# Linear attention with a gated feed-forward, one core: nine tokens per partition, no remainder tiles, 64x64 key-value products, and a new order of all engines

## The chip, the core and the metric

The kernel runs on one core of a Trainium2 chip. The metric is the time of one execution in microseconds of device time. Three timed runs of the kernel before gave 260.96, 260.99 and 261.04 us, median 260.99.

A core has five engines with a queue each: TensorE (PE, matrix products; the loading of its weights is listed apart as PEld), VectorE (DVE), ScalarE (ACT), GpSimd (POOL) and SyncE (SP). A queue runs its instructions in order; an instruction waits at its head until what it needs is there. Transfers are issued from SP, ACT or POOL, and all run on the same 16 DMA engines. Matrix products go to PSUM, which only PE, DVE and ACT reach; everything else lies in SBUF, 128 partitions wide.

## The reference, cut to what matters

```python
# q, k, v: (8 batches, 8 heads, 576 tokens, 64), f32
def phi(x):
    return np.where(x > 0, x, np.exp(x) - 1.0) + 1.0
q_p, k_p = phi(q), phi(k)
kv = np.einsum('bhsd,bhse->bhde', k_p, v)
z = np.sum(k_p, axis=2)
num = np.einsum('bhsd,bhde->bhse', q_p, kv)
den = np.einsum('bhsd,bhd->bhs', q_p, z)[..., None] + 1e-06
x = (num / den).transpose(0, 2, 1, 3).reshape(4608, 512)
a = x @ w1            # (512, 1024)
b = x @ w2            # (512, 1024)
h = a * b @ w3        # (1024, 1024)
out = h @ w_out       # (1024, 512)
```

Both kernels compute phi(x) as max(x + 1, min(exp(x), 1)) or, what is the same, min(exp(x), max(x, 0) + 1). Both multiply w3 and w_out first, into one 1024x512 matrix, so that each token takes three products instead of four: a, b and (a*b) @ (w3 @ w_out). All products are taken in bf16 with f32 sums.

## The kernel before, in words

**Tiles.** The 576 tokens of a batch are cut into 512, four to a partition (`NJ = 4`, tiles "J" of 128 tokens), and a remainder of 64 (`R`, tiles "R"; two batches share one). So q, k and v of a batch come as one load of 1 MB each and, for the remainder, two small loads of 64 KB each (`load_qkv`, L105; L111 is the small ones, L120 the large). The 4608 tokens make 36 tiles of 128; four tiles, whatever batch they are from, are a chunk of 512 tokens, and nine chunks go through the feed-forward.

**Attention, per batch.** `phi_exp` (ACT, L137), `phi_min` and `phi_max` (DVE, L141 and L162) make phi of q and k in bf16, in pieces of 1024 and 256 elements and, for the remainder, pieces of its own. `v_unit` (L171, L176) casts v into a tile with a column of ones beside each head, so that one product gives kv and z. `kv_half` (L181) multiplies for a pair of heads the two halves of the partitions separately (64 rows by 128 columns of the array, 130 columns moving), and DVE adds the two halves (L204). `kv_full` (L208) does the same at full height, for batch 0. `q_tr` (L302) transposes q on PE for batches 0 to 3, `qt_load` (L232) by a transposing transfer on SP for the others, and for the remainders. `nat_units` (L244) multiplies each transposed q tile with kv, head by head at half height (64 rows), takes the reciprocal of the denominators and scales (L271, L273, L275). The result is brought into the layout that the feed-forward needs, features on partitions, by `xt_tr` on PE (batches 1 and 3) or `xt_load` on SP. Batch 0 goes another way: `first_kvz` spreads kv and z into two block matrices, `first_nd` multiplies them with transposed q, 512 tokens at once, so that the result needs no transposing, and the reciprocal is taken on ACT as exp(-ln(x)).

**Feed-forward, per chunk.** `f_unit` (L379): for each of eight blocks of 128 features, four products into a_ps and four into b_ps (L371); ACT copies a_ps (L376), DVE multiplies with b_ps into ab (L377). `o_unit` (L386): eight products per tile of 128 tokens (L390), a copy on ACT or DVE (L393), and `o_store` on SP. `o_last` does the last tile in two halves (L417 to L420).

**Weights.** `load_w3`, `load_wo` and `load_w12` are issued from POOL and change f32 to bf16 on the way. `w3_tr` transposes w3 on PE (L454, copy L455), `wf_mm` multiplies with w_out (L464, copy L467).

**Order.** Nothing is scheduled by a program: `ORDER` (L470) is a list of steps, and each step appends its instructions to its engines' queues. `GATES` names six loads that wait for another one to be issued first. Letters: L, M, N load k, q, v; x, X exp; y, Y min; z, Z max; v cast; K kv; T, D transposing transfers; a, b transposes of q; A `nat_units`; P `xt_tr`; c to g, h, i, r the way of batch 0; E, C, B load w3, w_out, w1 and w2; w transposes w3; U, W multiply it with w_out; F, O, S, Q the feed-forward and its stores; a "+" moves a copy from ACT to DVE, or a load from SP to POOL. PSUM has eight banks: four for the feed-forward (tag "mm"), two tiles of two banks for attention ("at").

Of the kernel before, what the change touches and what calls it, by code (L numbers as in the profile page):

```python
# [13 lines left out]
P = 128  # L14
NCH = 512


@with_exitstack
def kernel(
# [10 lines left out]
):  # L30
    nc = tc.nc
    B, H, S, D = q.shape
    DM = H * D
    NTOK = B * S
# [3 lines left out]
    NJ = 4  # L38
    R = S - NJ * P
    JW = H * NJ * D  # L40
    RW = (H // 2) * D
    n_chunks = NTOK // NCH

    tile_of, order = {}, []
    for b in range(0, B, 2):
        for key in [("J", b, j) for j in range(NJ)] + [("J", b + 1, j) for j in range(NJ)] + [("R", b, 0)]:
            tile_of[key] = len(order)
            order.append(key)  # L50
        tile_of["R", b + 1, 0] = tile_of["R", b, 0]
# [5 lines left out]
    ldr = ctx.enter_context(tc.tile_pool(name="ldr", bufs=8))  # L57
    setup = ctx.enter_context(tc.tile_pool(name="setup", bufs=2))
    phi_p = ctx.enter_context(tc.tile_pool(name="phi", bufs=1))
    e_p = ctx.enter_context(tc.tile_pool(name="e", bufs=2))  # L60
    att = ctx.enter_context(tc.tile_pool(name="att", bufs=2))
    lr = ctx.enter_context(tc.tile_pool(name="lr", bufs=2))
# [5 lines left out]

    ident = consts.tile([P, P], BF16)
    mask = consts.tile([P, 2, 2, D], BF16)  # L70
# [5 lines left out]
    wo_sb = wpool.tile([P, FC, DM], BF16)  # L76
    wf_sb = wpool.tile([P, FC, DM], BF16)
    xt = wpool.tile([P, NT, KC, P], BF16)
    vt = wpool.tile([P, NJ, H, D + 1], BF16)
    vr = wpool.tile([P, H // 2, D + 1], BF16)  # L80

    def constants(part):
        if part == 0:
            make_identity(nc, ident)
        elif part == 1:

            nc.gpsimd.memset(mask, 0.0)
            nc.gpsimd.memset(mask[0:D, :, 0, :], 1.0)
            nc.gpsimd.memset(mask[D:P, :, 1, :], 1.0)
            nc.gpsimd.memset(eps, 1e-6)  # L90
            nc.gpsimd.memset(vt[:, :, :, D:D + 1], 1.0)
            nc.gpsimd.memset(vr[:, :, D:D + 1], 1.0)
        else:
            nc.vector.memset(zero, 0.0)

    def warm_up(n):

        ps = mm_ps.tile([P, NCH], F32, tag="mm", name="warm")
        for _ in range(n):
            nc.tensor.matmul(ps, zero[:, 0:P], zero, start=True, stop=True)  # L100


    raw = {}

    def load_qkv(name, src, b, part, alt=False):  # L105


        if part == 3:
            t = raw[name + "r", b] = ldr.tile([P, RW], F32, tag="ldr", name=f"{name}32r")
            for hh in range(2):  # L110
                (nc.gpsimd if alt else nc.sync).dma_start(  # L111
                    out=t[hh * R:(hh + 1) * R].rearrange("p (h d) -> p h d", d=D),
                    in_=src[b, hh * 4:(hh + 1) * 4, NJ * P:S, :].rearrange("h p d -> p h d"))
            return None
        if (name, b) not in raw:
            raw[name, b] = ld.tile([P, JW], F32, tag="ld", name=f"{name}32")
        t = raw[name, b]
        h0, h1 = ((0, 4), (4, 8), (0, 8))[part]
        W = NJ * D
        return nc.sync.dma_start(  # L120
            out=t[:, h0 * W:h1 * W].rearrange("p (h x) -> p h x", x=W),
            in_=src[b, h0:h1, 0:NJ * P, :].rearrange("h (p j) d -> p h (j d)", j=NJ))


    ph = {}

    es = {}

    def phi_exp(name, b, g):

        if g == 2:
            x, e = raw[name + "r", b], e_p.tile([P, RW], BF16, tag="er", name="er")
        else:
            x = raw[name, b][:, g * (JW // 2):(g + 1) * (JW // 2)]
            e = e_p.tile([P, JW // 2], BF16, tag="e", name="e", bufs=4)
        es[name, b, g] = x, e
        nc.scalar.activation(out=e, in_=x, func=AF.Exp)  # L137

    def phi_min(name, b, g):
        e = es[name, b, g][1]  # L140
        nc.vector.tensor_scalar_min(out=e, in0=e, scalar1=1.0)  # L141

    def phi_max(name, b, hp):

        if (name, b) not in ph:
            ph[name, b] = [None, None]
        if hp == KC:
            dr = ph[name, b][1] = phi_p.tile([P, RW], BF16, tag=name + "r", name=name + "r", bufs=3)
            todo = [(dr, *es[name, b, 2])]
        else:  # L150
            if hp == 0:
                ph[name, b][0] = phi_p.tile([P, KC, NJ, 2, D], BF16, tag=name + "j", name=name + "j")
            dj = ph[name, b][0]
            x, e = es[name, b, hp // 2]
            W = NJ * D
            todo = []
            for u in range(2):
                h = 2 * (hp % 2) + u
                todo.append((dj[:, hp, :, u, :], *(t[:, h * W:(h + 1) * W].rearrange(
                    "p (j d) -> p j d", d=D) for t in (x, e))))  # L160
        for out, x, e in todo:
            nc.vector.scalar_tensor_tensor(  # L162
                out=out, in0=x, scalar=1.0, in1=e, op0=ALU.add, op1=ALU.max)

    def copy_of(alt):
        return nc.vector.tensor_copy if alt else nc.scalar.copy

    def v_unit(b, i, alt=False):

        if i < 2:  # L170
            copy_of(alt)(  # L171
                out=vt[:, :, 4 * i:4 * i + 4, 0:D],
                in_=raw["v", b].rearrange("p (h j d) -> p j h d", h=H, j=NJ)[
                    :, :, 4 * i:4 * i + 4])
        else:
            copy_of(alt)(out=vr[:, :, 0:D], in_=raw["vr", b].rearrange("p (h d) -> p h d", d=D))  # L176


    kvs, qts, xns = {}, {}, {}

    def kv_half(b, g):  # L181


        kj, kr = ph["k", b]
        if g == 0:
            kvs[b] = att.tile([P, KC, 2, D + 1], BF16, tag="kv", name="kv")
        kvp = at_ps.tile([P, 2, 512], F32, tag="at", name="kvp")
        W = 2 * (D + 1)
        for i in range(2):
            hp = 2 * g + i  # L190
            steps = [(kj[:, hp, j].rearrange("p u d -> p (u d)"),
                      vt[:, j, 2 * hp:2 * hp + 2, :].rearrange("p h e -> p (h e)"), (0, 1))
                     for j in range(NJ)]
            steps.append((kr[:, i * P:(i + 1) * P],
                          vr[:, 2 * i:2 * i + 2, :].rearrange("p h e -> p (h e)"), (g,)))
            for n, (kk, vv, halves) in enumerate(steps):
                for r in halves:
                    rows = slice(r * R, (r + 1) * R)
                    nc.tensor.matmul(  # L199
                        kvp[:, r, i * W:(i + 1) * W], kk[rows], vv[rows],  # L200
                        start=(n == 0), stop=(n == (NJ if r == g else NJ - 1)))
        kvf = lr.tile([P, 2 * W], F32, tag="kvf", name="kvf")
        nc.scalar.copy(out=kvf, in_=kvp[:, 0, 0:2 * W])  # L203
# [4 lines left out]
    def kv_full(b, g):  # L208

        kj, kr = ph["k", b]  # L210
        if g == 0:
            kvs[b] = att.tile([P, KC, 2, D + 1], BF16, tag="kv", name="kv")
# [418 lines left out]
```

## Time and profile before

| | us |
|---|---|
| median of three runs | 260.99 |
| span of the profiled execution, first to last instruction | 258.1 |
| PE busy | 237.4 (92%) |
| DVE busy | 167.9 (65%) |
| ACT busy | 129.0 (50%) |
| POOL busy | 21.1 (8%) |
| 576 products of a and b | 150.0 |
| 266 recorded products of o | 63.2 |
| w3 @ w_out, 61 recorded products | 16.7 |
| HBM read, written | 38.80 MB, 9.44 MB |

The profiled execution's own time is told only by its span; the median of the runs lies 2.9 us above it. Busy time is the time in which at least one instruction of the group was running: products overlap in the pipeline, so a product of 512 columns is listed at 380 ns and costs 216 ns in a group. The granted clock was 0.999 over the span. The forty slices of section 2 of the page are 6.45 us each. In the table of stretches a row is: stretch, its length, then for each engine busy time and, in brackets, instructions, in the order PE, PEld, DVE, ACT, POOL (or the one engine asked for), then the granted clock, the DMA share and GB/s written.

### The profile page before, as it was taken

The page shows a single profiled execution, that of the slowest core. Times are in us where ns is not written, and L with a number is a line of the kernel's source. Part 1 is how long each engine was busy: PE and PEld are TensorE (multiplying, and loading weights), DVE is VectorE, ACT ScalarE, POOL GpSimd, SP SyncE. Part 2 cuts the span into 40 slices and gives each one's busy share as a digit, 9 for nine tenths or more (in the row PEclk, how much of TensorE's full clock was granted, in tenths as well). Part 3 has the DMA queues.
Part 4 walks back from the last instruction along what each step waited for, and adds up shares of the span by engine and source line. Part 5 has one row for each costly group of instructions (what it writes and reads, how often), then busy time and mean ns, then how long its engine had stood idle before and what let it go on. Part 6 is the DMA issues. An engine that isn't in the chain of part 4 may idle for free.

```text
span 258.1 us, 4507 instructions
## 1 busy us (share of the span) xinstructions
PE 237.4 (92%) x1656; PEld 116.2 (45%) x1673; DVE 167.9 (65%) x426; ACT 129.0 (50%) x205; POOL 21.1 (8%) x42
## 2 busy tenths in 40 slices
PE   1138999999999999999999999999999999999994
PEld 1124554545454454455444444444444444444442
DVE  0025787969978979997968589468866543423320
ACT  2048587858478664677353645726533203331421
POOL 8000765000101000000000000000000000000000
PEclk9999999999999999999999999999999999999999
DMA  6999999999898599939988975934980124003024
GB/s 100 200 257 378 316 229 245 208 334 307 302 291 250 87 340 215 307 104 253 211 193 245 369 160 123 248 99 131 218 220 26 34 57 124 0 37 125 3 82 163
DMA packets 70085, 48.98 MB, mean 190 GB/s; under 512 B 34416, under 2 KB 64368, under 8 KB 70064
## 3 DMA queue, kind: packets, MB, share of 16 engines
q1 hardware_dynamic: 63104, 42.54, 61.4%
q0 software_dynamic: 6816, 6.03, 14.1%
q8 instruction: 13, 0.21, 0.3%
q10 hardware_dynamic: 144, 0.13, 0.1%
q14 instruction: 8, 0.07, 0.1%
HBM read 38.80 MB, written 9.44 MB: 187 GB/s over the span
## 4 chain that ended last, share of the span: by engine, by line
PE 84%; DMA 8%; ACT 2%; SPq 1%; issue 1%; DVE 1%; DVEq 0%; POOLq 0%
PE a_ps L371 25%; PE b_ps L371 24%; PE o_ps L390 23%; DMA k<-in_k_dram 4%; DMA w3b<-in_moe_w_dram 4%; PE kvp L199 3%; PE wf_ps L464 3%; PE nd L265 3%; SPq L111 1%; PE tp L309 1%; PE w3p L454 1%; PE xtp L285 1%; PE o_ps L417 1%; DVE qj L162 1%; ACT e L137 0%
## 5 line engine op out<-in xcount | busy, mean ns | idle before, releaser
L371 PEld LDWEIGHTS <-w_sb 128*128 128x128 bf16 x576 | 54.2, 98 | 63.4 <-issue 0.5
L377 DVE TENSOR_TENSOR ab<-a_sb,b_ps 128x512 bf16<-128x512 f32 x72 | 49.0, 684 | 46.6 <-PE b_ps L371 35.4
L371 PE MATMUL a_ps<-xt,w_sb 128*128 128x512 bf16 x288 | 75.1, 380 | 0.1
L371 PE MATMUL b_ps<-xt,w_sb 128*128 128x512 bf16 x288 | 74.9, 379 | 0.0
L376 ACT COPY a_sb<-a_ps 128x512 f32<-128x512 f32 x72 | 41.9, 586 | 56.8 <-PE a_ps L371 55.6
L390 PE MATMUL o_ps<-wf_sb,ab 128*128 128x512 bf16 x266 | 63.2, 379 | 0.7
L390 PEld LDWEIGHTS <-ab 128*128 128x128 bf16 x280 | 26.7, 98 | 30.8
L393 ACT COPY o_sb<-o_ps 128x512 f32<-128x512 f32 x24 | 14.0, 583 | 30.7 <-PE o_ps L390 30.7
L162 DVE SCALAR_TENSOR_TENSOR kj<-k,e 128x256 bf16<-128x256 f32 x64 | 23.6, 417 | 0.1
L162 DVE SCALAR_TENSOR_TENSOR qj<-q,e 128x256 bf16<-128x256 f32 x64 | 23.4, 417 | 0.1
L141 DVE TENSOR_SCALAR e<-e 128x1024 bf16<-128x1024 bf16 x32 | 13.4, 420 | 14.2 <-ACT e L137 14.2
L137 ACT ACTIVATE e<-q 128x1024 bf16<-128x1024 f32 x16 | 16.7, 1058 | 9.3 <-DMA q<-in_q_dram 9.1
L454 PE MATMUL w3p<-ident,w3b 128*128 128x128 bf16 x64 | 6.1, 253 | 15.0 <-ACT w3t L455 8.0
L137 ACT ACTIVATE e<-k 128x1024 bf16<-128x1024 f32 x16 | 16.9, 1056 | 4.1 <-DMA k<-in_k_dram 2.7
L275 DVE TENSOR_TENSOR xn<-nd,r 128x512 bf16<-128x512 f32 x28 | 18.0, 686 | 0.0
L464 PE MATMUL wf_ps<-wo_sb,w3t 128*128 128x512 bf16 x61 | 16.7, 412 | 1.0 <-ACT w3t L455 0.8
L454 PEld LDWEIGHTS <-w3b 128*128 128x128 bf16 x64 | 4.9, 113 | 16.6 <-DMA w3b<-in_moe_w_dram 8.2
L393 DVE COPY o_sb<-o_ps 128x512 f32<-128x512 f32 x11 | 7.6, 688 | 6.4 <-PE o_ps L390 6.4
L171 ACT CAST vt<-v 128x1024 bf16<-128x1024 f32 x9 | 9.3, 1046 | 2.0 <-DMA v<-in_v_dram 2.0
L203 ACT COPY kvf<-kvp 128x260 f32<-128x260 f32 x14 | 5.3, 375 | 8.9 <-PE kvp L199 8.7
L464 PEld LDWEIGHTS <-w3t 128*128 128x128 bf16 x64 | 6.2, 104 | 7.8 <-issue 1.7
L199 PE MATMUL kvp<-vt,kj 64*128 64x130 bf16 x224 | 9.2, 217 | 0.0
(81 smaller groups left out, 163.5 us busy)
## 6 DMA issues: line engine op xcount, KB each, us to landing
out_dram<-o_sb SPq DMA_DIRECT2D x31, 256.0 KB, 3.2
k<-in_k_dram SPq DMA_DIRECT2D x7, 1024.0 KB, 8.6
q<-in_q_dram SPq DMA_DIRECT2D x7, 1024.0 KB, 8.2
v<-in_v_dram SPq DMA_DIRECT2D x6, 1024.0 KB, 7.4
w3b<-in_moe_w_dram POOLq DMA_DIRECT2D x8, 256.0 KB, 7.1
v<-in_v_dram SPq DMA_DIRECT2D x4, 512.0 KB, 8.5
w_sb<-in_moe_w_dram POOLq DMA_DIRECT2D x8, 256.0 KB, 11.3
out_dram<-o_sb SPq DMA_DIRECT2D x9, 128.0 KB, 2.4
```

The costliest lines, as they stand in the source:

```text
L137: nc.scalar.activation(out=e, in_=x, func=AF.Exp)
L141: nc.vector.tensor_scalar_min(out=e, in0=e, scalar1=1.0)
L162: nc.vector.scalar_tensor_tensor(out=out, in0=x, scalar=1.0, in1=e, op0=ALU.add, op1=ALU.max)
L199: nc.tensor.matmul(kvp[:, r, i * W:(i + 1) * W], kk[rows], vv[rows], start=(n == 0), stop=(n == (NJ if r == g else NJ - 1)))
L275: nc.vector.tensor_tensor(out=dst.rearrange("p (c u) e -> p u c e", u=2), in0=v4[:, :, :, 0:D], in1=r[0:n].unsqueeze(3).to_broadcast([n, 2 ...
L371: nc.tensor.matmul(ps, w[:, kc, f * P:(f + 1) * P], xt[:, 4 * c:4 * c + 4, kc, :], start=(kc == 0), stop=(kc == KC - 1))
L376: nc.scalar.copy(out=a_sb, in_=a_ps)
L377: nc.vector.tensor_mul(out=abs_[c][:, f, :], in0=a_sb, in1=b_ps)
L390: nc.tensor.matmul(o_ps, ab[:, f, m * P:(m + 1) * P], wf_sb[:, f, :], start=(f == 0), stop=(f == FC - 1))
L393: copy_of(alt)(out=o_sb, in_=o_ps)
L454: nc.tensor.transpose(tp[:, kc, :], raw["w3", i][:, kc * P:(kc + 1) * P], ident)
L464: nc.tensor.matmul(wfs[i], w3ts[i][:, kc, :], wo_sb[:, kc, :], start=(kc == 0), stop=(kc == FC - 1))
```

## The change

- **Nine tokens per partition.** 576 = 64 x 9: a batch's tokens lie on 64 partitions, nine in each, and the two heads of a pair on the two halves. There are no remainder loads; a partition's run is 2304 bytes. phi works on 1152 elements at a time: `phi_exp` on ACT, `phi_lin` (max(x, 0) + 1) and `phi_min` on DVE.
- **64x64 kv.** `kv_mm` gives each head and half its own quarter of the array; no halves are added afterwards. `kv_copy` puts kv on the diagonal of a block matrix whose rest is zero.
- **Full-height products.** `nat_mm` multiplies 128 rows with the block matrix, two heads at once.
- **One load queue.** All q, k and v loads are issued from POOL, in line with the weights; SP has only the transposing transfers and the stores. There are no gates.
- **Batches 0 and 1** take the direct way (`q_tr`, `kvz_copy`, `first_mm`, `first_recip`, `first_mult`), now in quarters of the array; the others get q transposed on SP, by halves (`q_load`), and x too (`x_load`); `xt_tr` is gone.
- A tile of 128 tokens now has two tokens of each of 64 partitions, so `f_mul` writes ab with the two interleaved, and a tile is stored by two transfers of 64 rows.
- **New order**, in finer steps: products, copies and the multiplication of the feed-forward are steps of their own, and 45 warm-up products (H) instead of 9 stand in it.

```diff
-    NJ = 4
-    R = S - NJ * P
+    NJ = 9
+    R = S // NJ
+    HW = NJ * D
+    NG = 4
...
-        return nc.sync.dma_start(
-            out=t[:, h0 * W:h1 * W].rearrange("p (h x) -> p h x", x=W),
-            in_=src[b, h0:h1, 0:NJ * P, :].rearrange("h (p j) d -> p h (j d)", j=NJ))
+        (nc.gpsimd if pool else nc.sync).dma_start(
+            out=raw[name, b][:, hs, :],
+            in_=src[b].rearrange("(hp u) (p j) d -> (u p) hp (j d)", u=2, j=NJ)[:, hs, :])
...
+    def phi_lin(name, b, c):
+        rs[name, b, c] = e_p.tile([P, 2, HW], BF16, tag="r", name="r", bufs=2)
+        nc.vector.tensor_scalar(
+            out=rs[name, b, c], in0=raw[name, b][:, 2 * c:2 * c + 2, :],
+            scalar1=0.0, scalar2=1.0, op0=ALU.max, op1=ALU.add)
+
+    def phi_min(name, b, c):
...
+        nc.vector.tensor_tensor(
+            out=ph[name, b][:, c].rearrange("p j a d -> p a j d"),
+            in0=es[name, b, c].rearrange("p a (j d) -> p a j d", j=NJ),
+            in1=rs[name, b, c].rearrange("p a (j d) -> p a j d", j=NJ), op=ALU.min)
...
+    def kv_mm(b, cs):
...
+        for c in cs:
+            for j in range(NJ):
+                for u in range(2):
+                    rows = slice(u * R, (u + 1) * R)
+                    for a in range(2):
+                        nc.tensor.matmul(
+                            kvps[b][a * D:(a + 1) * D, u, c * (D + 1):(c + 1) * (D + 1)],
+                            kk[rows, c, j, a, :], vt[rows, c, j, a, :],
+                            start=(j == 0), stop=(j == NJ - 1))
+
+    def kv_copy(b, a, alt):
+        rows = slice(a * D, (a + 1) * D)
+        copy_of(alt)(out=kvb[b % 2][rows, :, :, a, :],
+                     in_=kvps[b][rows, :, 0:2 * (D + 1)].rearrange("p u (c e) -> p u c e", e=D + 1))
+
+    def q_load(b, u):
...
+        nc.sync.dma_start(
+            out=qts[b][:, u].rearrange("p c j t -> p (c j) t"),
+            in_=ph["q", b][u * R:(u + 1) * R].rearrange("p c j a d -> p (c j a d)"), transpose=True)
+
+    def nat_mm(b, t):
+        nd = nds[b, t] = at_ps.tile([P, 2, NCH], F32, tag="at", name="nd")
+        n = P if t < NG else R
+        for u in range(2):
+            for c in range(2):
+                w = qts[b][:, u, c, 2 * t:2 * t + n // R, :].rearrange("p j t -> p (j t)")
+                nc.tensor.matmul(
+                    nd[0:n, u, 2 * c * (D + 1):2 * (c + 1) * (D + 1)], w,
+                    kvb[b % 2][:, u, c].rearrange("p a e -> p (a e)"), start=True, stop=True)
...
+    def first_mm(b, c, z):
+        t = nd1[b, c, z] = at_ps.tile([P, 2, NCH], F32, tag="at", name="nd1")
+        for a in range(2):
+            rows = slice(a * D, (a + 1) * D)
+            for u in range(2):
+                nc.tensor.matmul(t[u * D:(u + 1) * D, a, :], kvz[b, z][rows, u, c, :],
+                                 qts[b][rows, u, c, 0:NJ - 1, :].rearrange("p j t -> p (j t)"),
+                                 start=True, stop=True)
...
+    def f_mul(c, f):
...
+        nc.vector.tensor_tensor(
+            out=abs_[c][:, f].rearrange("p (m t g) -> p m g t", g=2, t=R),
+            in0=fsb[c, f].rearrange("p (m g t) -> p m g t", g=2, t=R),
+            in1=fps[c, f, 1].rearrange("p (m g t) -> p m g t", g=2, t=R), op=ALU.mult)
...
+    def o_store(c, m):
+        for g in range(2):
+            nc.sync.dma_start(out=rows_of(c, m, g), in_=o_sbs[c, m][g::2])
...
+    WCOL = (0, 256, 640, 1024)
+    WOC = (0, 2, 4, 6, 8)
```

The new order, its start and its end. le, lo, lw load w3, w_out, w1 and w2; lk, lq, lv load k, q, v (batch, half; half 2 is the whole); xk, yk, zk are exp, lin and min of k, xq, yq, zq of q; vc casts v; wt transposes w3, wc copies it, wm multiplies it with w_out, wd copies the result; qa and qb transpose q and copy it; K is kv, kz its copies for the direct way; e, er, em the direct way's products, reciprocal and multiplication, rm and rd those of its last 64 tokens; fa, fb the products of a and b, fc and fm the copy and the multiplication; h the products of a and b for one block together; O, oc, S, Q the output.

```diff
+ORDER = """
+i2 i1 le7 i0 H6 lk0.0+ lk0.1+ le6 lq0.0+ lv0.1+ wt7 lv0.0+ le2 H12 wc7+ lo3 xk0.0 yk0.0 lq0.1+ le4 yk0.1
+xk0.1 lo1 zk0.0 lo0 wt6 zk0.1 lo2 H13 wc6 yq0.0 i3 lw2 xq0.0 vc0.1 zq0.0 le1 lv1.1+ vc0.0+ qa0.0 le3 qb0.0+
+K0.0 lq1.1+ K0.1 wt2 kz0.0+ kz0.1 e0.0.1 wc2 H1 er0.0.1 e0.0.0 H13 yq0.1 xq0.1 em0.0.1 er0.0.0 lk1.1+ zq0.1
+lk1.0+ qa0.1 em0.0.0 le5 le0 qb0.1 wt4 lq1.0+ wm7.0.4 wc4 lv1.0+ e0.1.1 lw1 wm2.0.4 er0.1.1 wm4.0.4 er0.1.0
+rm0 wm7.4.8 rd0 e0.1.0 wm2.4.8 wd7 em0.1.1 wm6.0.4 em0.1.0 wd2+ wm6.4.8 fa0.5 wd6+ wt1 fc0.5 fa0.7 vc1.1+
...
+wm5.0.4 lv2.2+ xq1.0 fm0.6 lq3.2+ wm0.0.4 vc1.0+ lk2.2+ wm5.4.8 zq1.0 lk3.2+ wm0.4.8 wd5 fm0.5 qa1.0 wd0+
+K1.0 qb1.0+ K1.1 kz1.1 kz1.0+ fa0.2 e1.0.1 fc0.2 e1.0.0 er1.0.0 fa0.3 fa0.4 er1.0.1 em1.0.0 fb0.3 yq2.1
+fc0.4 e1.1.1 em1.0.1 xq2.0 fb0.2 yq2.0 e1.1.0 er1.1.1 fm0.2 fb0.4 zq2.0 fc0.3 em1.1.1 xq2.1 h0.0 fm0.4 h0.1
...
+fb8.3 fc8.3 fa7.7 fm8.3 fb7.7 fc7.7 fa8.5 fm7.7 fb8.5 fc8.5 O7.0 fm8.5 O8.0 oc7.0 S7.0 O8.1 oc8.0+ S8.0 O8.2
+oc8.1+ S8.1 O7.2 oc8.2 S8.2 O7.1 oc7.2+ S7.2 O7.3 oc7.1+ S7.1 Q8.3 oc7.3 S7.3
+"""
```

## The prediction

> **What bounds the kernel now.** I read the page's busy line and forty slices first, then three stretches of the span, the waits of TensorE, and the first 26 us in order of time.
>
> ```profile
> PE 237.4 (92%) x1656; PEld 116.2 (45%) x1673; DVE 167.9 (65%) x426; ACT 129.0 (50%) x205; POOL 21.1 (8%) x42
> ...
> PE   1138999999999999999999999999999999999994
> ```
> ```profile
> 0.00:29.20 29.20, 13.48 (x80) 7.69 (x82) 9.12 (x24) 12.93 (x16) 9.25 (x25) 1.00 1.02 250
> 29.20:254.40 225.20, 223.94 (x1577) 108.52 (x1591) 158.81 (x403) 115.69 (x188) 11.85 (x18) 1.00 0.74 183
> 254.40:258.10 3.70, 0.00 (x0) 0.00 (x0) 0.00 (x0) 0.37 (x1) 0.00 (x0) 0.90 0.31 112
> ```
> The first figure pair behind the length is PE. From 29.2 us to its last product at 254.4 us PE is busy 223.94 of 225.20 us: it stalls 1.3 us in all. So only three things can move the time: what is lost before 29.2 us, how much work PE has, and the 3.7 us behind its last product. The start is lost to waits:
>
> ```profile
> PE w3p L454 <- ACT w3t L455: 8.0, 1, 8.0
> PE w3p L454 <- DMA w3b<-in_moe_w_dram: 7.0, 3, 5.1
> ...
> 14.89 1.06 ACT L137 ACTIVATE e<-q 128x1024 bf16<-128x1024 f32 x1 [9.13 <-DMA q<-in_q_dram]
> 15.85 1.91 ACT L455 COPY w3t<-w3p 128x1024 bf16<-128x1024 bf16 x2
> ...
> 16.90 1.01 PE L454 MATMUL w3p<-ident,w3b 128*128 128x128 bf16 x8 [7.99 <-ACT w3t L455]
> ...
> 17.70 3.62 PE L464 MATMUL wf_ps<-wo_sb,w3t 128*128 128x512 bf16 x8
> ```
> PE is out of work from 8.9 to 16.9 us because the copy of the second transposed w3 block stands on ACT behind an exp that waits for q until 14.89 us; then eight 512-column products take 3.62 us, where a warm group of eight takes 1.73. PE's prices, warm, from the chain of waits between 66 and 82 us (start, length, what):
>
> ```profile
> 65.81 1.73 PE o_ps L390 x8
> 67.53 0.45 PE tp L309 x8
> 67.98 0.24 PE nd L265 x8
> ...
> 75.68 1.13 PE kvp L199 x36
> 76.81 0.97 PE a_ps L371 x4
> ...
> 78.64 0.35 PE nd L265 x16
> ```
> 216 ns per 512 columns; 56 ns per 128x128 transpose. Eight 64-row products of 65 columns take 0.24 us, sixteen 0.35: 14 ns each and 0.13 us to enter the half-height form. The a_ps behind such a group has 0.97 instead of 0.86: 0.11 to leave. kv: (1.13 - 0.13)/36 = 28 ns for 130 columns, about half of what the columns alone need (54 ns at 216/512), so two 64-row tiles run side by side.
>
> **The change, part by part.** The sum is made against the span, 258.1 us; the page gives no other time of its execution, and the runs' median, 260.99, lies 2.9 us above it, which I add at the end.
>
> PE work, unchanged: 856 products of 512 columns in the a, b and o groups (184.9), 16 half ones (1.8), 64 of w3 @ w_out (13.8), 64 transposes of w3 (3.6): 204.1 us.
>
> PE work, changed (before, after):
> - q transposes: 64 x 56 ns = 3.6; 36 (batches 0 and 1 only, nine each half) = 2.0. x transposes: 32 = 1.8; none.
> - kv: seven batches of 36 x 28 ns + 0.24 = 1.25, four of them split in two (1.49), and 2.0 for batch 0 (0.98 a half) = 11.7; now 72 products of 64x64 and 65 columns in each of 8 batches, mostly one block: 72 x 14 ns + 0.24 = 1.25, with a split or two 10.4. Bounds: 7 ns (four tiles side by side), 28 ns (one column half after the other) = 6 to 18.
> - numerator and denominator: before 0.46 + 0.46 + 0.35 = 1.27 in 7 batches = 8.9; now 16 products of 128x128 at 57 ns and a 64-wide tail (4 x 57 ns + 0.24) = 1.4 in 6 batches = 8.3.
> - the direct path: before 8 x 0.216 and a rest group, 2.1; now two batches of four groups, each four 64x64 products of 512 columns. No row shows four quarters at once. Ends: all four together 0.216 + 0.24 = 0.46, in turn 0.86 + 0.24 = 1.1 a group. The nearest row is kv's, where tiles that share no rows overlap fully; I take 0.46 for these and allow 0.67 (pairs). 8 x 0.46 + 2 rest groups (16 x 14 ns + 0.24) = 4.6; 9.7 at the far end.
> Sums 28.1 and 25.3, totals 232.2 and 229.4. (Before: 29.2 + 232.2 less the 7.9 done by then, below, + 1.3 = 254.8; the trace has 254.4.)
>
> [...]
>
> The start. All q, k, v loads go to POOL's queue, first block, then k, w3, q, v of batch 0, in an order that PE's warm-up groups (45 products instead of 9) are fitted into; SP issues only transposes and stores. What the loads bring per us:
>
> ```profile
> 3.50:7.50 4.00, 1.03 (x8) 1.00 1.07 160
> 20.00:25.00 5.00, 4.17 (x27) 1.00 1.11 375
> ```
> The last column is GB/s written. The first stretch has w3 casts (f32 read, bf16 written) and a little k: 320 read. The second is q, k, v: 375. So a w3 block or a w_out quarter (0.52 MB) takes 1.64 us, a half load of q, k or v (0.59 MB) 1.55, and the three w1/w2 pieces (1.6, 1.6 and 1.0 MB), between the two rows, 4.7, 4.7 and 3.1. The first w3 block landed at 5.02 with 1.64 of flow, so landing = 3.4 + flow. In the new order lo0, the w_out quarter that the first product needs, has four w3 blocks, six half loads and two other quarters ahead of it: 6.6 + 9.3 + 4.9 with its own = 20.8, so it lands at 24.1. The last of v1 follows 22.2 of flow later (a quarter, 4.7, four w3 blocks, six half loads), at 46.3; w1/w2 columns 256 up at 51.0, and behind q2 (3.1) the last columns at 57.2. The first w3 @ w_out product can start at 24.1; by then PE has done 32 w3 transposes 1.8, one and a half q sides 1.0, kv of batch 0 1.3 and two direct groups 0.9 = 5.0 us, so it has lost 19.1. At 29.2 before it had done 32 w3 transposes 1.8, 24 products 5.2, 16 q transposes 0.9 = 7.9, and lost 21.3. Gain 2.2. From 24.1 on, against the landings: up to K1 PE has the 13.8 of w3 @ w_out, 1.8 and 1.5 of transposes, 1.4 of direct groups and six f groups (5.2) = 23.7, so it is there at 47.8, as v1 is cast (46.3 + 1.5); 1.25 of kv, three f pairs 5.2 and four direct groups 1.8 later, at 56.1, h0 wants the last columns: 1.1 late. I add this 1.1.
>
> POOL's queue: 30 issues of q, k, v (12 small ones before), priced between w3's and w1/w2's, about 0.65 us:
>
> ```profile
> L445 POOL DMA_DIRECT2D w3b<-in_moe_w_dram x8: 536/568/687, 1.2 to 28.3; - x8
> ...
> L431 POOL DMA_DIRECT2D w_sb<-in_moe_w_dram x8: 740/767/790, 28.8 to 40.4; - x8
> ```
> They lie under 1.5 us of flow each, and up to eight loads stand ahead. Cost nothing while that holds. SP loses 64 load issues and gets 32 more stores (0.33 to 0.57 each) and 6 more transposes (1.2 to 5); it has slack.
>
> DVE and ACT: exp, lin and min go over 1152 elements. Exp at 1.16 us x 32 = 37 (was 16.9 + 16.7 + 6.5 = 40). lin, like the f32 cast of v (702 ns for 1024 elements): 0.77; min of two bf16 tiles has no row: 0.77 like the cast, which I take since both only touch SBUF, or 1.36 by the slope of the two-input rows (256 elements 417 ns, 512 elements 686). 32 x (0.77 + 0.77) = 49 against 70.5 for min and max before (68 at the far end). With the rest counted by rows DVE has 160 to 179 us against 183 of rows before (which overlap to 167.9 busy): under PE's 229, no path of its own. Writing ab interleaved by 64 tokens I cost at nothing (684 ns, as now; to 1.1 us if the stride costs as much again as 400 elements): PE's 1.73 us per pair of groups covers either.
>
> The end. Before, behind PE's last product: ACT copy 0.37, its store's issue 0.37, landing; 3.7 in all. In the new order ACT has Q8.3's copy and store ahead of the copy of o-tile 7.3, though that tile is ready 0.9 us earlier, and S7.3 follows on SP in two halves: 0.58 + 0.4 + 0.4 more = 1.4, so 5.1. Ends: 0.6 (copy alone) to 2.0.
>
> Sum: 24.1 + (229.4 - 5.0) + 1.3 (stalls as before) + 1.1 + 5.1 = 256.0; + 2.9 = 258.9 us.
>
> **The rivals.**
> - Quarters in turn (ends on the other side). Where the 64x64 products do not overlap by columns, kv costs 28 ns each (18.1, +7.7) and the direct groups 1.1 (9.7, +5.1): 271.7. Against: the 64-wide tail rows (64*64 form) already run at 14 ns. It decides from +2.1 us, that is 18 ns per kv product.
> - The single queue is short of loads. At 320 GB/s also for q, k, v a half load takes 1.85, and w1/w2 4.9, 4.9, 3.3: lo0 1.8 us later, v1 3.8, the last columns 5, which h0 waits out: 263.9. For: POOL's queue alone shows 320 read above. Against: those are casts, and rows of 2304 bytes are longer than before's 1024.
> [...]
> - DVE late in the start: min at 1.36 and the interleaved ab dearer. Between 36 and 48 us DVE has some 17 instructions in PE's way, four of them min: +2.4 us at K1; the 1.1 at h0 is then already spent: 260.2 to 262.
> - Better: loads at 390 and kv at 7 ns: 1.5 and 4 less, a part of it where PE waits anyway: 254 to 256.
>
> **How the numbers follow.** Forecast (256.5 to 260.4) 0.43; better 0.12; short of loads 0.18; DVE late 0.15; quarters in turn 0.08; POOL held up 0.04. Faster by over 0.2% (below 260.47; 0.2%, 0.5 us, is about what these runs can tell) takes the first two and a little of the fourth: 0.57; within 0.2%: 0.11, from the fourth and the forecast's edge; slower: 0.32. Range 254 to 266: it leaves out the last two cases and the edges of the others.
>
> **What would show it.** Right: first wf product at 23 to 25 us, PE busy over 222 us from there on, kv blocks of 72 at 1.2 to 1.3 us, direct groups of four at under 0.5, DVE under 165 us busy, 5 us behind the last product. Wrong: PE idle behind POOL's loads between 30 and 60 us (load landings above 58 us for the last w1/w2 piece), kv blocks over 1.5 us, min at 1.36, waits of PE for DVE ab in the middle.

## The result, and the profile after

The changed kernel takes 275.69 us (median of four runs, 272.28 to 277.34); the kernel before took 260.98 beside it. The ratio is 1.0487, 95% interval 1.043 to 1.0543: slower by some 5%, where 258.9 was forecast and the range ended at 266. (A ratio leaves out the runs that lie more than 1.5% above the fastest of their kernel; a median is taken over all.)

The page of the changed kernel, its span, the busy line of PE, PE and its clock in forty slices of 6.83 us, and what the DMA engines moved:

```profile
span 273.2 us, 4642 instructions
...
PE 239.0 (87%) x1826; PEld 115.1 (42%) x1841; DVE 151.0 (55%) x281; ACT 122.1 (45%) x175; POOL 37.9 (14%) x56
...
PE   6589999999700299999999999999999999999991
...
PEclk9899999999955599999999999999999999999998
...
GB/s 129 337 271 205 343 326 291 339 392 312 326 133 119 255 96 233 297 329 274 237 185 275 242 197 89 57 40 42 152 171 159 10 41 152 11 0 2 57 151 99
```

From the fourth slice on, all but four and the last are as full as before. From 72 us on PE stands still for the better part of three slices, its clock falls to a half in three, and the DMA engines move 133 and 119 GB/s where they had moved 326 just ahead: the transfers are not missing, they are slow. The stretches around it (busy time and instructions by engine, then clock, DMA share, GB/s):

```profile
24.50:72.40 47.90, 47.19 (x434) 22.43 (x436) 35.20 (x57) 34.75 (x51) 15.79 (x20) 1.00 1.12 325
72.40:93.70 21.30, 1.02 (x5) 0.29 (x3) 1.17 (x2) 2.28 (x4) 0.75 (x1) 0.59 1.16 179
93.70:266.80 173.10, 172.56 (x1213) 82.99 (x1224) 103.46 (x204) 71.71 (x106) 6.00 (x8) 0.99 0.59 142
266.80:273.20 6.40, 0.81 (x8) 0.49 (x5) 0.42 (x1) 0.96 (x2) 0.00 (x0) 0.80 0.27 95
```

Outside the 21.3 us PE idles some 1.3 us between its first product of w3 @ w_out, at 24.7, and its last product, at 266.8. What it waits for is one line of its waits:

```profile
PE nd L264 <- DMA qt<-q: 20.3, 1, 20.3
```

The chain of waits names the transfer and what follows it (start, length, what):

```profile
25.53 0.34 PE nd L327 x4
...
47.70 0.71 PE kvp L239 x71
...
59.36 34.30 DMA qt<-q
...
93.71 1.05 PE nd L264 x8
94.76 1.71 PE a_ps L376 x4
```

The second half of batch 2's q, turned by a transposing transfer of SP (`q_load`, step T2.0), is issued at 59.36 and lands 34.30 us later. The first products behind it run at half clock: 1.05 for eight where 0.47 is usual, 1.71 for four where 0.86 is; some 1.5 us are lost so. All such transfers of q, on SP's queue by start, length of issue and number:

```profile
57.97 17.10 SPq L252 DMA_TRANSPOSE qt<-q  x2
...
77.42 16.33 SPq L252 DMA_TRANSPOSE qt<-q  x2
...
118.17 16.59 SPq L252 DMA_TRANSPOSE qt<-q  x4
...
168.07 3.53 SPq L252 DMA_TRANSPOSE qt<-q  x2
...
188.05 3.48 SPq L252 DMA_TRANSPOSE qt<-q  x2
```

The same pair takes 3.5 us to issue at 168 and 188 us, when no q, k or v is loaded any more, and 16 to 17 us at 58 and 77 us. At 118 us it is slow again, but nothing waits for it. From issue to landing, least, median and longest of these twelve:

```profile
DMA to landing us min/median/max: 4.1/7.2/34.3
```

The stores of `o_store` (L411), on the same ring of SP, show it too: 2.1 us at the median, 18.8 at the longest.

Against the sum of the prediction the span of 273.2 us comes out so: 0.6 more at the start, +20.3 for this wait, +1.5 for the cold clock, +1.3 behind the last product (6.4 for 5.1), and, as what remains, 6.5 less in PE's work and stalls: 256.0 + 17.2.

### The profile page after: what moved, and what is told of

The parts are those of the page before. It is cut to its first block, busy times and chain, and to the rows that moved or that the text cites. A ratio compares the mean times of both kernels' runs of the same rounds, so it can differ in the third digit from the quotient of the medians.

```text
span 273.2 us, 4642 instructions
## 1 busy us (share of the span) xinstructions
PE 239.0 (87%) x1826; PEld 115.1 (42%) x1841; DVE 151.0 (55%) x281; ACT 122.1 (45%) x175; POOL 37.9 (14%) x56
## 3 DMA queue, kind: packets, MB, share of 16 engines
q0 software_dynamic: 12032, 33.56, 43.9%
## 4 chain that ended last, share of the span: by engine, by line
PE 74%; DMA 16%; ACT 3%; DVE 2%; POOL 2%; issue 1%; ACTq 0%; POOLq 0%; DVEq 0%
PE a_ps L376 21%; PE b_ps L376 21%; PE o_ps L397 20%; DMA qt<-q 13%; PE wf_ps L195 5%; DMA v<-in_v_dram 4%; PE nd L264 3%; PE kvp L239 2%; ACT rc L335 1%; ACT rc L336 1%; PE w3p L185 1%; DVE xt L340 1%; POOL k L149 1%; DVE r L213 0%; DVE vt L226 0%
## 5 line engine op out<-in xcount | busy, mean ns | idle before, releaser
L264 PE MATMUL nd<-kvb,qt 128*128 128x130 bf16 (+1 forms) x120 | 11.2, 228 | 20.3 <-DMA qt<-q 20.3
L209 ACT ACTIVATE e<-k 128x1152 bf16<-128x1152 f32 x16 | 18.1, 1162 | 7.0 <-DMA k<-in_k_dram 7.0
L264 PEld LDWEIGHTS <-qt 128*128 128x128 bf16 (+1 forms) x120 | 8.6, 103 | 26.6 <-DMA qt<-q 20.8
L209 ACT ACTIVATE e<-q 128x1152 bf16<-128x1152 f32 x16 | 18.2, 1163 | 0.4 <-DMA q<-in_q_dram 0.4
L195 PE MATMUL wf_ps<-wo,w3t 128*128 128x512 bf16 x61 | 14.5, 380 | 0.1
L139 PE MATMUL warm<-zero 128*128 128x512 bf16 x44 | 12.6, 445 | 1.2 <-DVE zero L131 1.2
L213 DVE TENSOR_SCALAR r<-k 128x1152 bf16<-128x1152 f32 x16 | 11.8, 753 | 3.0 <-DMA k<-in_k_dram 3.0
L149 POOL DMA_DIRECT2D k<-in_k_dram x10 | 7.4, 740 | 43.8 <-ACT vt L226 26.2
L149 POOL DMA_DIRECT2D v<-in_v_dram x10 | 8.8, 878 | 32.7 <-ACT e L209 9.3
L213 DVE TENSOR_SCALAR r<-q 128x1152 bf16<-128x1152 f32 x16 | 12.1, 770 | 2.0 <-DMA q<-in_q_dram 2.0
L220 DVE TENSOR_TENSOR q<-e,r 128x1152 bf16<-128x1152 bf16 x16 | 11.9, 751 | 1.7 <-ACT e L209 1.6
## 6 DMA issues: line engine op xcount, KB each, us to landing
w3b<-in_moe_w_dram POOLq DMA_DIRECT2D x8, 256.0 KB, 10.5
```

The costliest lines, as they stand in the source:

```text
L149: (nc.gpsimd if pool else nc.sync).dma_start(out=raw[name, b][:, hs, :], in_=src[b].rearrange("(hp u) (p j) d -> (u p) hp (j d)", u=2, j=N ...
L195: nc.tensor.matmul(wfs[i], w3ts[i][:, kc, :], wos[0][:, kc, :], start=(kc == 0), stop=(kc == FC - 1))
L209: nc.scalar.activation(out=es[name, b, c], in_=raw[name, b][:, 2 * c:2 * c + 2, :], func=AF.Exp)
L213: nc.vector.tensor_scalar(out=rs[name, b, c], in0=raw[name, b][:, 2 * c:2 * c + 2, :], scalar1=0.0, scalar2=1.0, op0=ALU.max, op1=ALU.add)
L264: nc.tensor.matmul(nd[0:n, u, 2 * c * (D + 1):2 * (c + 1) * (D + 1)], w, kvb[b % 2][:, u, c].rearrange("p a e -> p (a e)"), start=True, st ...
```

## The experiments

The theory (A): transposing transfers on SP's ring get little of the DMA engines while loads of q, k and v run on another ring. Before, all large loads came from SP itself, in the written order with the transposes; now all come from POOL, up to five buffers ahead. Rivals: B, that too much is loaded at that time in the new order, whatever the ring; C, that the new form of the transposing transfer (two of 64 rows by 1152) is slow in itself; D, that the loads are late too and the transposes only hide it, so that taking their wait away gives little. E and F come up below: E, that the transposes are slow at that place for another reason; F, that it is something of POOL's ring alone.

**1. Whole loads from SP again.** Only the queue is undone, for batches 2 to 7; order, forms and everything else stay.

```diff
-            load_qkv(op[1], src[op[1]], x, y, alt)
+            load_qkv(op[1], src[op[1]], x, y, alt and x < 2)
```

> One part undone: the 18 whole loads of q, k and v (batches 2 to 7) are issued from SP, in the places where the order has them; the loads of batches 0 and 1 and the weights stay on POOL. Theory A (two rings): q's transposes sit in SP's ring and give way, packet by packet (256 bytes), to POOL's loads (4608 bytes). In one ring they come in line instead: the transposes of q2 land within 15 us of their issue instead of 34.3, TensorE's wait for them falls from 20.3 us to under 6, time 254 to 261. Theory B (too much is loaded at that time, whatever the ring): the wait stays over 15 us, time over 270. Theory C (the new form, halves of 64 partitions, is slow): as B.

Measured: 263.11 us (261.04 to 264.91), ratio to before 1.0075 (1.0028 to 1.0121), so 12.6 us less than the changed kernel. The wait for q is gone; PE's largest waits behind the start are now:

```profile
PE a_ps L376 <- DMA xt<-xn: 4.8, 1, 4.8
...
PE b_ps L376 <- DMA w_sb<-in_moe_w_dram: 1.9, 1, 1.9
```

So the queue of the loads makes most of the loss, and neither the amount loaded nor the form does (B, C fall). It is over the 254 to 261 that A gave, by these two waits and some 2.2 us of cold clock behind the first, which A had not foreseen: x of batch 2, the next transposing transfer, is late in its turn.

**2. q of batches 2 and 3 turned by PE**, as in batches 0 and 1, with the loads left on POOL: the transfers that were waited for no longer exist.

```diff
- ... em1.1.0 T2.1 rm1 vc2.0 h1.1 fm0.0 T2.0 fa1.0 ... T3.0 yk2.0 xk2.0 O0.0 zk2.1 T3.1 ...
+ ... em1.1.0 qa2.0 qb2.0 rm1 vc2.0 h1.1 fm0.0 qa2.1 qb2.1+ fa1.0 ... qa3.0 qb3.0 yk2.0 xk2.0 O0.0 zk2.1 qa3.1 qb3.1+ ...
```

> q of batches 2 and 3 is transposed on TensorE like that of batches 0 and 1 (36 products and four copies more), its four transposing transfers are gone; all else as in the changed kernel. All theories of the transposes: the wait of 20.3 us goes with them and the 1.5 us of half clock behind it; TensorE gets 36 x 56 ns = 2.0 us more: 275 - 21.8 + 2.0 = 255. A rival D (the loads of batches 2 and 3 are late too, the transposes only hide it): kv of batch 3 or the next nd waits instead, time over 262.

Measured: 269.26 us (266.65 to 274.62), ratio 1.023 (1.0174 to 1.0286; from two of the four runs). The expected 255 was a miss. The time is the one that D gave (over 262), but not for D's reason: behind the start PE waits for no load. In the chain of waits the next transposing transfer takes the place of the one removed:

```profile
85.63 20.03 DMA xt<-xn
```

The next loads of POOL's queue (k at 82.89 and 87.50 us, v at 95.99) stand beside batch 2's x, and PE waits 11.7 us for it. The trouble moves to the transposing transfer that comes next; it does not belong to q's.

**3. The kernel before, with its whole loads (1 MB, `part == 2`) issued from POOL.**

```diff
-        return nc.sync.dma_start(
+        return (nc.gpsimd if part == 2 else nc.sync).dma_start(
```

> One part alone, in the kernel before: its 20 whole loads of 1 MB (batches 1 to 7) are issued from POOL; the halves of batch 0 and the remainders stay where they are. Theory A: its transposing transfers lose their place in line; those of q and x (landing 4.9 and 4.6 us in the median, 11.2 at most) take over 8 us in the median and over 15 at most, and TensorE begins to wait for them; time 262 to 275. Theories B and C: transposes as before, time 259 to 262.

Measured: 260.91 us (nine of ten runs at 260.16 to 261.82, one at 270.68), ratio 0.9982 (0.9961 to 1.0003): no change, a miss for A as it stood. The transfers are slower at the median, but not at their longest; the twelve transposes of q (L242), from issue to landing, before and here:

```profile
DMA to landing us min/median/max: 2.3/4.9/11.2
```
```profile
DMA to landing us min/median/max: 2.3/7.6/9.3
```

Up to 9.3 us were hidden; 34.3 could not be. In this kernel PE turns q of batches 0 to 3, and SP issues one small transfer of the remainder at a time next to the loads (1.2 us of issue each), four large ones of q only after 100 us. So a second ring of loads alone is not enough. That it also needs large transposing transfers, which PE waits for in the stretch in which the loads are dense, is argued from the trace and was not tried by itself.

**4. The second experiment, and o-tile 7.3 copied and stored ahead of the halves of 8.3.**

```diff
-oc8.1+ S8.1 O7.2 oc8.2 S8.2 O7.1 oc7.2+ S7.2 O7.3 oc7.1+ S7.1 Q8.3 oc7.3 S7.3
+oc8.1+ S8.1 O7.2 oc8.2 S8.2 O7.1 oc7.2+ S7.2 O7.3 oc7.1+ S7.1 oc7.3 S7.3 Q8.3
```

> As the run with q2 and q3 on TensorE, and the copy and store of output tile 7.3 moved ahead of the last tile in the order. The prediction put 1.4 us on that place: from TensorE's last product to the end of the span 5.0 us instead of 6.4, time 1.4 us under that run. Rival: the end is set by the stores before it on SP, and nothing moves.

Measured: 269.48 us (262.67 to 282.79, nine runs), ratio 1.008 (1.0038 to 1.0122; from the two shortest runs, 262.67 and 263.61). Behind PE's last product come 3.9 us (257.9 to 261.8) instead of 6.4: the swap gives 2.5 where 1.4 was expected. In the middle the wait for x stays, 6.6 us in the profiled run, which is one of the two shortest. The nine runs lie 20 us apart; the others have no trace.

```profile
PE a_ps L376 <- DMA xt<-xn: 6.6, 1, 6.6
```

**5. The loads held back.** The changed kernel; each whole load waits until the transposing transfer written ahead of it has landed.

```diff
-    raw = {}
+    raw, turned = {}, []
...
-        (nc.gpsimd if pool else nc.sync).dma_start(
+        ins = (nc.gpsimd if pool else nc.sync).dma_start(
...
+        if turned and True:
+            tc.add_manual_dep(ins.ins, turned[-1].ins.name, mybir.DependencyInfo(
+                mybir.DependencyClass.Sync, mybir.DependencyReason.SCHED_ONLY), reason="load order")
...
-        nc.sync.dma_start(out=dst, in_=src, transpose=True)
+        turned.append(nc.sync.dma_start(out=dst, in_=src, transpose=True))
```

(and the same `turned.append` around the transfer in `q_load`.)

> The changed kernel; every whole load of q, k or v on POOL's queue now waits until the transposing transfer of SP that stands ahead of it in the written order has landed; nothing is left out. After the start at most two loads (some 7 us of flow) run beside a transposing transfer. Theory A (transposing transfers on SP's ring are starved of DMA time by loads on POOL's ring): batch 2's q lands in under 8 us instead of 34.3, PE's wait of 20.3 us for it is gone, the clock does not drop: 253 to 258 us; up to 262 if two loads still hold back the x of batch 2. Rival D (the loads themselves are needed earlier than that, so that holding them back only turns the wait for transposes into a wait for loads): PE waits for DVE or ACT behind q, k or v, 262 to 275. Rival E (the transposes are slow at that place for another reason): 270 or more with the wait for qt in place.

Measured: 263.35 us (262.96 to 269.03), ratio 1.0083 (1.0052 to 1.0115), just over the upper end that A gave for a late x. No wait for q is left, and the longest of q's landings is 13.0 us instead of 34.3. What is left is again x of batch 2, for which PE waits 7.8 us; in the chain of waits, and POOL's loads (start, length, what, and in brackets the idle time before and its end):

```profile
84.12 14.55 DMA xt<-xn
```
```profile
83.88 0.75 POOL L149 DMA_DIRECT2D k<-in_k_dram  x1 [12.26 <-DMA qt<-q]
84.62 0.75 POOL L149 DMA_DIRECT2D q<-in_q_dram  x1
86.39 0.75 POOL L149 DMA_DIRECT2D k<-in_k_dram  x1 [1.03 <-ACT o_sb L405]
```

Three loads, 3.5 MB or some 11 us of flow (an estimate, at the 325 GB/s of the changed kernel from 24.5 to 72.4 us), are let go at 84 to 87 us, since nothing but the first half of that x stands between them in the order; the second half, issued with them at 84.12, lands at 98.67, when they are through. Rival E falls, and D does too: behind the start PE waits for no load, there was a second place of the same kind.

**6. Rows of half the length**, to give the loads smaller packets.

```diff
-        (nc.gpsimd if pool else nc.sync).dma_start(
-            out=raw[name, b][:, hs, :], in_=...[:, hs, :])
+        for xs in (slice(0, HW),) if part < 2 else (slice(0, HW // 2), slice(HW // 2, HW)):
+            nc.gpsimd.dma_start(
+                out=raw[name, b][:, hs, xs], in_=...[:, hs, xs])
```

> The changed kernel with every whole load of q, k or v split in two by columns, so that its rows are 1152 bytes instead of 2304; all on POOL's queue as before, nothing left out. If the DMA engines take packets of the rings in turn (A1), smaller load packets give the 256-byte packets of the transposes a larger share: the landing of batch 2's q falls from 34.3 to 15 to 24 us, PE's wait from 20.3 to some 5 to 12, 260 to 268 us. If the engines share by bytes or are simply full (A2), nothing changes: 270 to 278.

Measured: 276.99 us, ratio 1.0474 (1.0406 to 1.0543), and the same wait as in the changed kernel:

```profile
PE nd L265 <- DMA qt<-q: 20.4, 1, 20.4
```

It tells nothing between turns (A1) and bytes (A2), because the packets did not change. POOL's queue, after and here (packets, MB, share of the DMA engines):

```profile
q0 software_dynamic: 12032, 33.56, 43.9%
```
```profile
q0 software_dynamic: 12320, 33.56, 43.4%
```

But this run has the cleanest stretch to count in, since no store runs from 62 to 78 us. The packets that the trace has as started on all 16 DMA engines, by stretch:

```
us        4608 bytes (loads)   256 bytes (transposes)
62 to 66         256                 284
66 to 70         294                 334
70 to 74         291                 327
74 to 78         208                 230
```

1.11 to 1.14 transposing packets start for each load packet, 1.12 in all, which is close to the one to one that taking turns packet by packet would give: 1175 in 16 us, 73 per us. In the fifth experiment it is 1.06 (505 beside 476, 90 to 96 us).

How far that explains the 34.3 us can be counted in the changed kernel's own trace. Taking away four transposing transfers of q took 4608 packets of 256 bytes from it (27648 in the changed kernel, 23040 in the second experiment), 1152 each; batch 2's two are 2304. At 73 per us that would be some 31 us, close to 34.3, but by luck. The first transfer's 1152 start from 62.1 to 75.5 us beside 859 load packets, at 317 GB/s in all. The second's start from 75.5 to 89.1 us, and there the loads hardly run either: 280 load packets, 121 GB/s in all. So turns, if that is what the counts show (1.34 to one in the first stretch), account for about the first 13.5 us, and the second 13.5 belong to the slow stretch that is left open at the end of this document.

**7. Loads of batches 2 and 3, and v of batch 4, from ACT's queue**, a third ring.

```diff
-        (nc.gpsimd if pool else nc.sync).dma_start(
+        q = nc.scalar if b in (2, 3) or (name, b) == ("v", 4) else nc.gpsimd
+        q.dma_start(
```

> The changed kernel with the loads of batches 2 and 3 and of v of batch 4 issued from ACT's queue, a third ring, instead of POOL's; nothing left out. If what hurts is a second ring of loads beside the transposes, whichever engine fills it (A1, A2), the wait for batch 2's q stays, at half its size or more (10 to 20 us): 263 to 275. If it is something of POOL's ring alone (F), the wait is gone as with the loads on SP: 253 to 262. ACT's own issues cost some 9 x 0.6 us on ACT, which is busy 45 per cent.

Measured: 284.13 us (277.75 to 297.35). Worse than the changed kernel; PE waits 8.7 us for q and 13.1 for x. The two transfers in the chain:

```profile
64.12 22.27 DMA qt<-q
...
97.69 20.88 DMA xt<-xn
```

284 lies above the 263 to 275 expected: both transfers are late here, and PE waits another 3.8 us for ACT's copy of kv, which comes at 51.86 us behind two issues of k that hold ACT from 44.23 for 7.11 us. It does not settle F, because POOL still issued three loads in the stretch (q at 68.37 us, k at 72.18, q at 78.75). The packets by ring, in two stretches in which only one of the two rings has loads running:

```
us        loads                        256 bytes (transposes)
66 to 72   543 of 2304 bytes (ACT)          1402
74 to 80   396 of 4608 bytes (POOL)          454
```

Beside ACT's loads 234 transposing packets start per us, beside POOL's 76, as in the sixth experiment. The 1152 packets of the first transfer take 2.8 us here (66.6 to 69.4) where they took 13.5 in the changed kernel, and while x is waited for, from 97.7 to 118.6 us, all loads are POOL's. PE's wait for q, too, falls behind the last of ACT's loads (77.7 to 86.4 us). So both waits are made beside POOL's loads, and F stands. ACT's load packets are half as long (2304 bytes; the same holds for the loads on SP in the first experiment), so their length (A1) may be the reason as well as the ring, though 2.6 transposing packets for each load packet are more than one to one. Length and ring were not told apart.

**8. Loads held back, q of batches 2 and 3 on PE, and the swap at the end**: the edits of 2, 4 and 5 together; against 4 it differs by the held loads, and by the two halves of batch 3's q standing in the other order.

> The loads held back as in the first run of this set, q of batches 2 and 3 transposed by PE as in batches 0 and 1 (+1.3 us of PE), and o-tile 7.3 copied and stored ahead of the halves of 8.3. Nothing left out. Theory A: no wait for transposes above 3 us, last product at 247 to 249, 3.9 behind it, 1.9 outside the span: 252 to 256. Rival D (loads held back come late): 260 to 270. Rival E: a wait of 5 us or more for xt of batch 2 stays: 258 to 266.

Measured: 255.76 us (254.77 to 257.16), ratio to before 0.9802 (0.9751 to 0.9852): faster than both kernels, 13.7 less than the fourth experiment at the median, and 6.9 less than that one's shortest run. PE and its clock in slices, and its waits of 0.8 us and more:

```profile
PE   6969999998979989999999999999999999999993
...
PEclk9999999999999999999999999999999999999999
```
```profile
PE o_ps L400 <- ACT a_sb L386: 1.7, 1, 1.7
PE kvp L242 <- DVE vt L229: 1.4, 1, 1.4
PE warm L139 <- DVE zero L131: 1.2, 1, 1.2
PE w3p L188 <- DMA w3b<-in_moe_w_dram: 1.1, 2, 0.9
PE a_ps L379 <- DMA xt<-xn: 0.8, 1, 0.8
```

The 6.6 and 11.7 us that PE waited for x with q of these batches on PE have become 0.8, and the clock does not fall. The 254.1 us of its span are within 2 us of the 256.0 that the prediction's sum gave for the changed kernel, with 36 transposes on PE more and the end 2.5 shorter.

**9 and 10. Four, and eight, transfers for each late load**, again to make packets smaller, by single rows of 2304 and 1152 bytes.

```diff
+        view = src[b].rearrange("(hp u) (p j) d -> (u p) hp (j d)", u=2, j=NJ)
+        late = b > 3 or (name, b) == ("v", 3)
+        n = 1    # 2 in the tenth
+        for hp in range(4) if late else (hs,):
+            for x in range(n):
+                xs = slice(x * HW // n, (x + 1) * HW // n)
+                nc.gpsimd.dma_start(out=raw[name, b][:, hp, xs], in_=view[:, hp, xs])
```

> The changed kernel; the loads of v of batch 3 and of all of batches 4 to 7 are issued in four transfers each, one per pair of heads' row of 2304 bytes, so that a packet of POOL's queue can no longer hold two such rows (4608 bytes, as it still did with the split by columns). Nothing left out. Turn-taking (A1: while loads flow, the DMA engines take about one 256-byte packet of a transposing transfer per load packet, 80 per us at 4608 bytes; the two transfers of batch 2's q are 2304 packets, 29 us): with 2304 bytes twice as many, so batch 2's q lands in 15 to 20 us instead of 34.3, PE's wait for it falls from 20.3 to 2 to 8, 257 to 266 us. If the transposes are slow beside loads whatever their packets (A2), the landing stays above 28 us and the time at 270 to 280.

> As the run before, each row once more split by columns: eight transfers per load, packets of 1152 bytes; POOL then issues a load in some 6 us, 196 GB/s at most. Nothing left out. Turn-taking (A1): four times as many transposing packets per byte of load, and gaps between the loads: batch 2's q lands in under 12 us, PE waits under 3 us for it; 254 to 262 us, unless the slower issue makes a load late (then PE waits for DVE or ACT, and the time is up to 266). A2: landing above 28 us, 270 to 280.

Measured: 291.42 us for the ninth (284.45 and 298.4), 267.61 for the tenth (267.48 and 267.75). Neither changed the packets: POOL's queue still has 4608-byte ones, 12656 and 13488 for the same 33.56 MB. So A1's forecast for shorter packets on POOL's ring stayed untried. The ninth is worse than the changed kernel (waits of 18.0 for q, 8.1 for x): from 70 to 76 and from 86 to 96 us both sides are slow, at 69 to 139 GB/s, and why is open. In the tenth POOL's loads come more slowly: with eight issues of 0.5 us for a load and waits between them, only 71 load packets start from 66 to 72 us, and 1802 transposing ones beside them.

```profile
PE a_ps L380 <- DMA xt<-xn: 4.6, 1, 4.6
...
PE nd L268 <- DMA qt<-q: 1.2, 1, 1.2
```

That fits the held loads: the transposes go through when POOL's loads pause. What is left of the loss is x of batch 2 again, and smaller waits behind (2.6 us for a copy of kv, 1.8 for ab).

**11. The edits of 1, 2 and 4 together**: loads on SP, q of batches 2 and 3 on PE (batch 3's halves in the order of the eighth), the swap.

> Three single edits together: the whole loads of batches 2 to 7 issued from SP, in the written order with the transposes, q of batches 2 and 3 transposed by PE, o-tile 7.3 stored ahead of 8.3. Nothing left out. Theory A: on one ring a transpose waits only for the loads that stand ahead of it: no wait above 5 us, last product at 248 to 251, 3.9 behind it and 1.9 outside: 253.5 to 258. Rival: SP's issues of loads wait for buffers with the transposes queued behind them, and batch 2's x is late by more than the 4.8 us of the first run: 259 to 266.

Measured: 258.07 us (257.26 to 259.99, nine runs), ratio 0.9908 (0.9875 to 0.9941). At the upper end of A's 253.5 to 258, with no wait for a transposing transfer among its large ones:

```profile
PE b_ps L376 <- DMA w_sb<-in_moe_w_dram: 3.1, 1, 3.1
PE o_ps L397 <- ACT a_sb L383: 1.7, 1, 1.7
```

On SP's ring the loads of batches 2 and 3 now run beside POOL's weights, and the last columns of w1 and w2 come 3.1 us late.

## Why the prediction was wrong, point by point

- **What failed** is the last sentence on the queues: "SP loses 64 load issues and gets 32 more stores (0.33 to 0.57 each) and 6 more transposes (1.2 to 5); it has slack." The sentence counts SP's time and puts nothing on its transfers. What the move took away was the one ring on which loads and transposes had been issued in turn; with the loads on POOL's ring the packets of both start in the same microseconds (1152 beside 859 from 62.1 to 75.5 us), and batch 2's q took 34.3 us, where such a transfer took 4.1 at the least. The term that was missing is 20.3 us of wait and 1.5 of cold clock. The loads on SP again (263.11, q's longest landing 11.0 us) and the loads held back on POOL (no wait for q left) both took it away. Some 13.5 of the 34.3 us are put down to turns with the loads, by the counts of packets; why both sides are slow in the rest is open, and so is whether loads on another ring than POOL's would do the same (the seventh experiment). And the queue alone does not do it: the kernel before lost nothing by it (the third).
- It was missing because the load queue was priced as a supply: are the loads in time for PE. They are; between 24.7 and 72 us PE waits for none, and the rival "short of loads" did not come. The prediction did not ask what the loads, being early, do to the transfers beside them, and no rival covered that. Four loads were issued between 60 and 75 us (v, q and k of batch 4, q of batch 5) that no step of the order uses before the second transfer of batch 2's x has been issued.
- **The start** was right: first product of w3 @ w_out at 24.7 us, forecast 24.1.
- **Quarters of 64x64** were better than forecast: 72 kv products in 0.71 us, 10 ns each, for 1.25; near the 7 ns that was the lower bound. Over the seven blocks behind the start that is 3.8 us less. A direct group takes 0.34 to 0.41 for 0.46. The rival "quarters in turn" is refuted.
- **DVE**: min at 751 ns for 0.77, lin at 753 to 770 for 0.77; busy 151 us, under the 160 to 179. The interleaved ab costs 731 ns for 684 and is hidden. "DVE late" did not come.
- **POOL held up** (by DVE, 0.04 of the chances) did not come either: its loads of q, k and v are issued in 0.75 us at the median, 0.1 more than priced, and three of the thirty took longer (1.04 to 1.29 us). What made those three longer is not shown; PE's one wait behind a cast of v is 0.2 us. POOL's long idle times are waits for buffers (the longest, 26.2 us, ends with a cast of v on ACT).
- **h0 waiting 1.1 us for the last columns** did not come in the changed kernel.
- **The end**: 6.4 us for 5.1, from the copy of 7.3 behind Q8.3 on ACT, as forecast, with ACT's two issues of 0.56 and 0.50 ahead of it.
- **The 2.9 us added at the end** were too many: in nearly all runs the time lies 1.7 to 2.1 us above its own span (274.93 for 273.2 here). The 2.9 set a median beside the span of one shorter execution.
- So the rest of the sum was 4.6 us too high: without the wait and the cold clock it would be 273.2 - 21.8 = 251.4 us of span, against 256.0, chiefly by the quarters (3.8 in kv) and the 1.1 at h0. That is worked out; the run that comes nearest to it is the eighth, 254.1.

## What to carry to other kernels

When a transfer moves to another queue, price what it does to the transfers that stay behind, not only whether it arrives in time: here q's transposing transfers landed within 11.0 us with the loads on their own ring (the first experiment), and one of them, 1152 packets of 256 bytes, took 34.3 us with the loads on another. Loads that run far ahead of their use were not free; holding them back behind the transfer that is needed sooner took the time from 275.69 to 263.35 us (the fifth). And when a wait is taken away, ask which transfer of the same kind comes next: twice here the trouble only moved from q to x.

## What the hardware showed that was not expected

- Four 64x64 quarters multiply at 10 ns per product of 65 columns (72 in 0.71 us), where a product of 512 columns at full height takes 216 ns: less than half of what the columns would need in turn (65/512 of 216 is 27).
- Beside POOL's loads the transposing packets start nearly one for one, though the sizes differ 18 times: 1.06 to 1.15 packets of 256 bytes for each of 4608 in three runs (the fifth, sixth and seventh), in the sixth while the loads go on at 300 GB/s (1049 packets in 16 us); 1.34 in the changed kernel (1152 beside 859, 62.1 to 75.5 us).
- Beside loads from ACT's ring, in packets of 2304 bytes, the transposing packets started three times as often: 234 per us for 76 (the seventh).
- Something beside those counts stays open. From 77 to 92 us in the changed kernel both sides are slow: 133 and 119 GB/s in all, and a transposing packet takes 126 to 189 ns between 78 and 86 us where it takes 18 alone (94 to 98 us). In the changed kernel a second pair of transposes and stores had been issued by then, but neither is needed: in the second experiment it comes beside a transposing transfer of x (69 to 104 GB/s, 98 to 104 us), and in the ninth it is there at 70 us, when the first pair and POOL's loads are all that is issued. What makes it is open.
- Splitting POOL's loads into two, four or eight transfers did not make its packets smaller than 4608 bytes in the records, while the same loads on SP or ACT went in packets of 2304 bytes, one row each (in the first experiment SP's queue has 9504 packets more than in the changed kernel, for 21.2 MB more).
